# A second place for the loaded keys and queries of every second head pair

## The chip, the cores and the metric

The kernel runs on one core of a Trainium2 chip. The core has five instruction streams that run beside each other and wait for one another by semaphores: TensorE (PE: matrix products and transposes; PEld are its weight loads), VectorE (DVE), ScalarE (ACT), GpSimd (POOL) and SyncE (SP), which here issues every transfer between DRAM and the on-chip memory SBUF, in one queue. Each stream runs its instructions in order: what stands behind a waiting instruction waits too. The metric is the device time of one execution in microseconds (us).

## The reference

`reference.py` computes causal attention with a gated linear memory, and feeds its result to a two-layer network; everything is fp32. Inputs: q, k, v of shape (4, 8, 576, 64), that is 4 batches, 8 heads, 576 positions, 64 features; `M_prev` (4, 8, 64, 64), `z_prev` (4, 8, 64), `beta` (8), `w_in` (512, 2048) and `w_out` (2048, 512).

```
scores = where(causal, -1e9, q @ k.T / 8);  a = softmax(scores)
qp     = phi(q)                       # phi(x) = max(x, 0) or exp(x) - 1, plus 1
mem    = (qp @ M_prev) / (qp . z_prev + 1e-6)
attn   = g * mem + (1 - g) * (a @ v)  # g = sigmoid(beta), one number per head
x      = attn as (2304 tokens, 512);  h = x @ w_in
out    = (h * sigmoid(1.702 * h)) @ w_out
```

## The kernel before, in words

**Exact products.** A product of fp32 numbers is built from three products of a fast, shorter format (fp32r): each operand is split into a high part (a rounded copy, made by ACT) and a low part (value minus high part, made by POOL or DVE), and high*high, high*low and low*high are summed in PSUM.

**Pairs.** The 32 heads go as 16 pairs (0 to 15): two heads of one batch fill the 128 partitions. Batch 0 is pairs 0 to 3. The first 256 queries of all of batch 0 are done ahead, by `first_queries`, whose tiles lie in the pool `first`; pairs 0 to 3 then do the other 320 queries, and their memory part is one plain fp32 product. The room of `first` is given back after it, to the pools of the converted weight blocks (`w1_6` to `w1_15`); a tile in that room waits until the last reader of the tiles that it covers is done.

**What a pair goes through.** In `plan_prep`: the transposed keys (576 columns) and queries (384 or 640 columns) are loaded into one tile `kqr` of the pool `ldp`, which has one buffer for it (`load_kq`, L352 to L357); ACT makes their high part, tile `hi`, one buffer too (`split_hi`); POOL subtracts, `lok` and `loq` (its last instruction on `kqr`); ten SBUF-to-SBUF transfers stack high and low parts into two weight tiles `W0`, `W1` (L402 to L411), so that one pass of PE does what else were three. In `plan_attend`: PE makes the scores (`ps<-W`; the last 64 rows, the tail, directly from the parts: `ps<-hi`, `ps<-lok,hi`, `ps<-hi,loq`, the last readers of `hi`), DVE takes the maximum (L506), ACT the exponential (L512), POOL scales (L515), PE transposes (`pt`), ACT and DVE copy out (`e`), and PE multiplies by the values (`po<-e,vs`) and the memory (`po<-qpt,ms`). The sum is x, transposed. `load_vq` loads values, memory (`mr`), queries in the other layout (`qr`) and z (`zb`); for pairs 0 to 3, ACT writes the gated memory to the tile `ms` (two buffers, `mplain`), which PE reads.

**Blocks.** w_in comes as 16 blocks of 128 columns of d_ff, as raw 64-bit words: 512 KB each into one of the two buffers `wraw` of the pool `cnv` (L164). ACT scales the upper words (L172), DVE puts the bits together in three operations (L179, L180, L182), ACT copies the high part `wi` and POOL subtracts the low part. Blocks 0 to 5 are converted in front, 6 to 15 while the first pairs run. From about 410 us the two `wraw` buffers take w_out's raw words (L861, L865); the first two of these are loaded as soon as the buffers are free.

**First product.** h = x @ w_in runs as "fill" between the pairs' work: for each chunk of x (256 tokens, then 320, then 288 each) and each block, 12 matmuls `pm<-xh,wi` and `pm<-xl,wi`; the result is copied by ACT or DVE to `hk` (three buffers) and stored in DRAM (`gd<-hk`, L738). The second product (`acc`, L949) starts near 480 us and ends the program.

**What sets the order.** Work is put into slots: `at(slot, prio, fn)` notes a piece of work, `step()` issues those of a slot by priority and then as many first-product matmuls as `PACE` grants. Pair p starts at slot `K0[p]` (0, 7, 14, 21, then every 8); its preparation at `K0[p]-8`. The tile framework's scheduler then orders each engine's instructions by its own estimates; the order on each engine is fixed when the program is built.

Of the kernel before, what the change touches and what calls it, by code (L numbers as in the profile page):

```python
# [8 lines left out]
F32 = mybir.dt.float32  # L9
# [6 lines left out]
B, H, S, D = 4, 8, 576, 64  # L16
NP = H // 2
# [3 lines left out]
NB = DFF // 128  # L21
NK = DM // 128
SQ = 640
# [6 lines left out]
def f32(ap):  # L30
    return ap.bitcast(F32)
# [3 lines left out]
def tile_attention_memory_moe(ctx, tc, kq, vq, mem, zz, beta, w_in, w_out, out):  # L35
    nc = tc.nc
    CH = 288
    NCH = S // CH
    MB = 1
# [3 lines left out]
    W0 = 6  # L43
    CONV = [-7, -6, -5, -3, -1, 1, 3, 5, 7, 9]
    PSUM = bass.MemoryType.PSUM

    def pool(stack, name, bufs=1, **kw):
        return stack.enter_context(tc.tile_pool(name=name, bufs=bufs, **kw))

    attn = ExitStack()  # L50
    left = ExitStack()
    cst = pool(ctx, "cst", side="left")
    mop = pool(left, "mop", 2, side="left")
    cnv = pool(left, "cnv", side="left")
    w1 = [pool(left, f"w1_{k}", side="left") for k in range(W0)]
# [4 lines left out]
    ldp = pool(attn, "ldp", side="right")  # L60
    att = pool(attn, "att", side="right")
# [19 lines left out]
    def at(slot, prio, fn):  # L81
        assert slot > state["slot"], (slot, state["slot"])
        state["seq"] += 1
        events.setdefault(slot, []).append((prio, state["seq"], fn))
# [12 lines left out]
    def copy(eng, dst, src, scale=None):  # L97
        if eng == "A":
            kw = {} if scale is None else {"scale": scale}
            nc.scalar.activation(out=dst, in_=src, func=AF.Copy, **kw)  # L100
        elif eng == "V":
            if scale is None:
                nc.vector.tensor_copy(dst, src)
            else:
                nc.vector.tensor_scalar(out=dst, in0=src, scalar1=scale, scalar2=None, op0=ALU.mult)
        else:
            nc.gpsimd.tensor_copy(dst, src)

    def tt(eng, dst, a, b, op):
        (nc.vector if eng == "V" else nc.gpsimd).tensor_tensor(out=dst, in0=a, in1=b, op=op)  # L110

    def sub(eng, dst, src, hi):
        tt(eng, dst, src, f32(hi), ALU.subtract)
# [12 lines left out]
    for r in range(2):  # L126
        v = maskt[64 * r:64 * r + 64, CH - 64:CH]
# [7 lines left out]
    gt = cst.tile([128, NP], F32, name="gt")  # L135
# [206 lines left out]
    pairs = [(b, c) for b in range(B) for c in range(NP)]  # L342
    raws = {}
# [3 lines left out]
    K0 = [STEP * p for p in range(MB * NP)]  # L347
    K0 += [(K0[-1] + 8 if K0 else 0) + 8 * p for p in range(len(pairs) - len(K0))]

    def load_kq(p):  # L350
        kqr = ldp.tile([128, S + SQ], F32, name="kqr")
        b, c = pairs[p]  # L352
        if b < MB:
            nc.sync.dma_start(kqr[:, :S], kq[b, c, :, :S])
            nc.sync.dma_start(kqr[:, S:S + 384], kq[b, c, :, S + 256:])
        else:
            nc.sync.dma_start(kqr, kq[b, c])  # L357
        raws[p] = {"kq": kqr}

    def load_vq(p):  # L360
        b, c = pairs[p]

        vr = (att.tile([128, 5, 128], F32, name="vs", bufs=2) if b < MB else ldp.tile([128, 5, 128], F32, name="vr"))
        nc.sync.dma_start(vr, vq[b, c, :, 0])
        mr = ldp.tile([128, 2, D], F32, name="mr")
        nc.sync.dma_start(mr, mem[b * NP + c])
        qr = ldp.tile([128, 5, 128], F32, name="qr")
        t = 2 if b < MB else 0
        nc.sync.dma_start(qr[:, t:], vq[b, c, :, 1, t:])
        zb = ldp.tile([128, 128], F32, name="zb")  # L370
        nc.sync.dma_start(zb, zz[b, c:c + 1, :].to_broadcast([128, 128]))
        raws[p].update(v=vr, m=mr, q=qr, z=zb)

    def plan_prep(p):
        b, c = pairs[p]
        s0 = K0[p] - 8
        P = prep[p] = {}
        rest = b < MB
        T0 = 2 if rest else 0
        qo = 256 if rest else 0  # L380

        def split_hi():
            kqr = raws[p]["kq"]
            P["hi"] = att.tile([128, S + SQ], F32R, name="hi")
            copy("A", P["hi"][:, :S + SQ - qo], kqr[:, :S + SQ - qo])

        def split_lo_k():
            P["lok"] = att.tile([128, S], F32R, name="lok")
            sub("P", P["lok"], raws[p]["kq"][:, :S], P["hi"][:, :S])

        def split_lo_q():
            P["loq"] = att.tile([128, SQ], F32R, name="loq")
            n = SQ - qo
            sub("P", P["loq"][:, :n], raws[p]["kq"][:, S:S + n], P["hi"][:, S:S + n])

        def stack_hi():
            P["W"] = [att.tile([128, S + 1024 - 2 * qo], F32R, name=f"W{h}", bufs=2) for h in range(2)]
# [21 lines left out]
                P["vs"][:, :, :, 0])  # L419

        def mplain():
            P["ms"] = att.tile([128, 2 * D], F32, name="ms", bufs=2)
            copy("A", P["ms"], raws[p]["m"].rearrange("p h d -> p (h d)"), gt[:, c:c + 1])

        def msplit():
            P["ms"] = att.tile([128, 2, 2, D], F32R, name="ms", bufs=2)
# [42 lines left out]
        def qev():  # L469
# [6 lines left out]
            for pt, a, n in ((P["pt"][0][:, qo:], qo, 512 - qo), (P["pt"][1], 512, 64)):  # L476
                copy("A", qh[:, a:a + n], pt[:, :n])
                sub("V", ql[:, a:a + n], pt[:, :n], qh[:, a:a + n])

        at(s0 + 1, 50, split_hi)  # L480
        at(s0 + 3, 50, split_lo_k)
        at(s0 + 3, 51, split_lo_q)
        at(s0 + 3, 52, stack_hi)
        at(s0 + 4, 52, stack_lo)
        if rest:
            at(s0 + 7, 51, mplain)
        else:
            at(s0 + 6, 55, vhi)
            at(s0 + 7, 50, vlo)
            at(s0 + 7, 51, msplit)  # L490
# [6 lines left out]
        at(s0 + 12, 21, qtr)  # L497
        at(s0 + 13, 31, qev)
        if p + 1 < len(pairs):
            at(K0[p + 1] - 11, 60, lambda: load_kq(p + 1))  # L500
            at(max(K0[p + 1] - 8, s0 + 8), 60, lambda: load_vq(p + 1))

    def softmax_max(pieces):
        nm = sml.tile([128, 2], F32, name="nm")
# [296 lines left out]
            for blk in range(W0):  # L801
                conv_in(blk)
    first.close()
    w1 += [pool(left, f"w1_{k}", side="left", reuse_waits="tile") for k in range(W0, NB)]
    load_kq(0)
    load_vq(0)
    for p in range(NPAIRS):
        plan_prep(p)
        plan_attend(p)
# [158 lines left out]
    k = 0  # L968
# [118 lines left out]
```

## Time and profile before

| | us |
|---|---|
| three executions | 673.61, 668.46, 672.34 |
| their median | 672.34 |
| the profiled execution, own time | 669.38 |
| its span in the trace | 667.6 |
| PE busy (share of the span) | 608.9 (91%) |
| DVE busy | 473.5 (71%) |
| ACT busy | 426.8 (64%) |
| POOL busy | 276.4 (41%) |
| granted TensorE clock, mean | 0.993 |

Times of rows are microseconds from the start of the span. What lies around the span is 669.38 - 667.6 = 1.8 us. An idle time in front of an instruction stands in brackets, with what ended it; the releaser is inferred from semaphores, so where it names a piece of work that was done long before, it was another. Busy time of engines other than PE matters only where PE, or a chain that PE waits for, waits for them.

### The profile page before, as it was taken

The page shows a single profiled execution, that of the slowest core. Times are in us where ns is not written, and L with a number is a line of the kernel's source. Part 1 is how long each engine was busy: PE and PEld are TensorE (multiplying, and loading weights), DVE is VectorE, ACT ScalarE, POOL GpSimd, SP SyncE. Part 2 cuts the span into 40 slices and gives each one's busy share as a digit, 9 for nine tenths or more (in the row PEclk, how much of TensorE's full clock was granted, in tenths as well). Part 3 has the DMA queues.
Part 4 walks back from the last instruction along what each step waited for, and adds up shares of the span by engine and source line. Part 5 has one row for each costly group of instructions (what it writes and reads, how often), then busy time and mean ns, then how long its engine had stood idle before and what let it go on. Part 6 is the DMA issues. An engine that isn't in the chain of part 4 may idle for free.

```text
span 667.6 us, 12447 instructions
## 1 busy us (share of the span) xinstructions
PE 608.9 (91%) x4032; PEld 578.2 (87%) x4032; DVE 473.5 (71%) x1117; ACT 426.8 (64%) x975; POOL 276.4 (41%) x304
## 2 busy tenths in 40 slices
PE   4588799899987899999999999889989999999997
PEld 3477687699976799999989999789989999999997
DVE  5977776677587767776667745983878469658944
ACT  4676556677488866775876655744794865776441
POOL 3746554876376955664675321670710000000000
PEclk9999899999999999999999999999989999999999
DMA  8959868875678848667665136855752660672001
GB/s 243 277 146 262 241 181 213 220 200 159 184 182 234 197 153 224 185 172 233 168 183 148 55 94 213 268 181 170 233 197 88 196 190 1 180 211 83 24 2 71
DMA packets 72048, 114.50 MB, mean 172 GB/s; under 512 B 8240, under 2 KB 52272, under 8 KB 71984
## 3 DMA queue, kind: packets, MB, share of 16 engines
q1 hardware_dynamic: 71984, 113.71, 58.7%
q8 instruction: 32, 0.52, 0.3%
q14 instruction: 32, 0.26, 0.1%
HBM read 62.87 MB, written 26.69 MB: 134 GB/s over the span
## 4 chain that ended last, share of the span: by engine, by line
PE 62%; DVE 11%; ACT 9%; DMA 9%; issue 5%; POOL 2%; SPq 1%; DVEq 0%; ACTq 0%; POOLq 0%
PE acc L949 24%; PE pm L91 18%; PE po L91 7%; PE pt L95 6%; PE ps L91 4%; DMA gd<-hk 3%; DMA xl<-xd 2%; DVE st L110 1%; DMA fm<-in_mem_dram 1%; DMA xd<-xf 1%; DVE ps L506 1%; ACT a L512 1%; ACT oh L100 1%; DVE ol L110 1%; ACT wo L100 1%
## 5 line engine op out<-in xcount | busy, mean ns | idle before, releaser
L91 PE MATMUL pm<-xh,wi 128*128 128x288 f32 (+2 forms) x1024 | 220.4, 304 | 13.7 <-ACT hk L100 7.1
L91 PEld LDWEIGHTS pm<-xh,wi 128*128 128x128 f32 x1024 | 165.6, 189 | 20.1 <-ACT hk L100 9.8
L949 PE MATMUL acc<-oh,wo 128*128 128x384 f32 x672 | 159.6, 339 | 4.5 <-ACT oh L100 4.2
L91 PE MATMUL pm<-xl,wi 128*128 128x288 f32 (+2 forms) x512 | 151.7, 299 | 0.2 <-DVE xl L110 0.2
L949 PEld LDWEIGHTS acc<-oh,wo 128*128 128x128 f32 x672 | 121.1, 189 | 6.3 <-ACT oh L100 6.3
L110 DVE TENSOR_TENSOR ol<-g,oh 128x768 fp32r<-128x768 f32 x84 | 81.4, 981 | 49.1 <-ACT oh L100 47.3
L515 POOL TENSOR_SCALAR a<-a,sm,g 128x512 f32<-128x512 f32 (+3 forms) x112 | 72.7, 661 | 69.1 <-DVE sm L554 30.3
L949 PE MATMUL acc<-ol,wo 128*128 128x384 f32 x336 | 99.4, 338 | 0.1
L100 ACT ACTIVATE oh<-g 128x768 fp32r<-128x768 f32 x84 | 70.3, 840 | 43.2 <-PE acc L949 41.8
L91 PEld LDWEIGHTS pm<-xl,wi 128*128 128x128 f32 x512 | 96.6, 189 | 0.9 <-DVE xl L110 0.4
L512 ACT ACTIVATE a<-ps,nm 128x512 f32<-128x512 f32 (+3 forms) x112 | 60.3, 541 | 34.5 <-DVE nm L506 32.2
L506 DVE CUSTOM_DVE_ANT_0 ps<-ps,mask 128x256 f32<-128x256 f32 (+4 forms) x144 | 69.4, 495 | 15.6 <-PE ps L91 9.5
L91 PE MATMUL po<-e,vs 128*128 128x320 f32 (+3 forms) x416 | 74.7, 304 | 1.7 <-ACT e L100 1.5
L110 DVE TENSOR_TENSOR e<-pt,e 128x320 fp32r<-128x320 f32 (+1 forms) x120 | 55.9, 486 | 23.3 <-ACT e L100 22.3
L100 ACT ACTIVATE e<-pt 128x320 fp32r<-128x320 f32 (+4 forms) x136 | 55.2, 437 | 26.4 <-PE pt L95 12.9
L91 PEld LDWEIGHTS po<-e,vs 128*128 128x128 f32 x416 | 63.0, 189 | 6.0 <-ACT e L100 1.8
L949 PEld LDWEIGHTS acc<-ol,wo 128*128 128x128 f32 x336 | 62.3, 189 | 1.0 <-DVE ol L110 1.0
L91 PE MATMUL ps<-W 128*128 128x512 f32 (+3 forms) x224 | 58.6, 343 | 3.5 <-ACT a L512 1.0
L95 PE MATMUL pt<-ident,a 128*128 128x128 f32 x296 | 56.6, 272 | 1.5 <-ACT a L512 1.5
L100 ACT ACTIVATE hk<-pm 128x288 f32<-128x288 f32 (+2 forms) x84 | 33.7, 407 | 28.0 <-PE pm L91 16.1
L912 ACT ACTIVATE g<-g 128x768 f32<-128x768 f32 x48 | 40.0, 842 | 14.6 <-DMA g<-gd 10.4
L95 PE MATMUL pt<-ident,at 128*128 128x128 f32 x160 | 40.7, 279 | 6.7 <-ACT a L512 3.0
(147 smaller groups left out, 1020.1 us busy)
## 6 DMA issues: line engine op xcount, KB each, us to landing
g<-gd SPq DMA_DIRECT2D x48, 384.0 KB, 3.7
gd<-hk SPq DMA_DIRECT2D x96, 144.0 KB, 2.7
wraw<-in_w_in_dram SPq DMA_DIRECT2D x16, 512.0 KB, 4.4
wraw<-in_w_out_dram SPq DMA_DIRECT2D x16, 512.0 KB, 4.6
kqr<-in_kq_dram SPq DMA_DIRECT2D x12, 608.0 KB, 5.4
W<-hi SPq DMA_DIRECT2D x24, 272.0 KB, 3.5
W<-loq SPq DMA_DIRECT2D x48, 128.0 KB, 3.4
W<-lok SPq DMA_DIRECT2D x32, 144.0 KB, 3.4
```

Source lines behind the costliest of these rows:

```text
L91: nc.tensor.matmul(out, l, r, start=start, stop=stop)
L95: nc.tensor.transpose(out, in_, idn)
L100: nc.scalar.activation(out=dst, in_=src, func=AF.Copy, **kw)
L110: (nc.vector if eng == "V" else nc.gpsimd).tensor_tensor(out=dst, in0=a, in1=b, op=op)
L506: nc.vector.tensor_tensor_reduce(out=ps, in0=ps, in1=mk, op0=ALU.add, op1=ALU.min, scale=-0.125, scalar=1e38 if j == 0 else nm[:, j - 1:j] ...
L512: nc.scalar.activation(out=a, in_=ps, func=AF.Exp, scale=-1.0, bias=nm, accum_out=sm)
L515: (nc.vector if eng == "V" else nc.gpsimd).tensor_scalar(out=a, in0=a, scalar1=r, scalar2=gcol, op0=ALU.mult, op1=ALU.mult)
L912: nc.scalar.activation(out=t, in_=t, func=AF.Gelu_apprx_sigmoid)
L949: nc.tensor.matmul(acc[b, j][:, :QN], W[2 * p + kk][:, WPART[i], sp, 128 * j:128 * j + 128], mv[:, kk], start=first and p + kk == 0 and sp ...
```

## The change

**Keys and queries.** `load_kq` is called at slot max(K0[p+1]-16, 10) where it was K0[p+1]-11, and at -7 for pairs 1 and 2. The even pairs keep `kqr`. Pair 1's goes into a new pool `kqx`, which is laid where block 15's weights will be (the pool `w1_15` is opened only at slot 9, when `kqx` is closed). The odd pairs from 3 on take two tiles (keys, queries) from the two `wraw` buffers. For the odd pairs keys and queries come in two transfers, and `split_hi` becomes two ACT copies for pairs 3, 5, 7 ... 15.

**Values and memory.** `load_vq` is cut into `load_q` (priority 60) and `load_v` (61). For pairs 0 to 3 the memory is loaded straight into the tile `ms`, and `mplain` scales it there; so the load itself has to wait until PE has read what the pair two before had in that buffer.

```diff
     def load_kq(p):
-        kqr = ldp.tile([128, S + SQ], F32, name="kqr")
         b, c = pairs[p]
-        if b < MB:
-            nc.sync.dma_start(kqr[:, :S], kq[b, c, :, :S])
-            nc.sync.dma_start(kqr[:, S:S + 384], kq[b, c, :, S + 256:])
+        n = 384 if b < MB else SQ
+        if p % 2 and p > 1:
+            k, q = [cnv.tile([128, w], F32, name="wraw", bufs=2) for w in (S, n)]
+        else:
+            kqr = (ldp if p % 2 == 0 else kqx["pool"]).tile([128, S + (SQ if p % 2 == 0 else n)], F32, name="kqr")
+            k, q = kqr[:, :S], kqr[:, S:S + n]
+        if b < MB or p % 2:
+            nc.sync.dma_start(k, kq[b, c, :, :S])
+            nc.sync.dma_start(q, kq[b, c, :, S + SQ - n if b >= MB else S + 256:])
         else:
             nc.sync.dma_start(kqr, kq[b, c])
...
-    def load_vq(p):
+    def load_q(p):
...
+    def load_v(p):
+        b, c = pairs[p]
+        vr = (att.tile([128, 5, 128], F32, name="vs", bufs=2) if b < MB else ldp.tile([128, 5, 128], F32, name="vr"))
+        nc.sync.dma_start(vr, vq[b, c, :, 0])
+        mr = (att.tile([128, 2, D], F32, name="ms", bufs=2) if b < MB else ldp.tile([128, 2, D], F32, name="mr"))
+        nc.sync.dma_start(mr, mem[b * NP + c])
...
-            copy("A", P["hi"][:, :S + SQ - qo], kqr[:, :S + SQ - qo])
+            if raws[p]["kq"] is not None:
+                copy("A", P["hi"][:, :S + SQ - qo], raws[p]["kq"])
+            else:
+                copy("A", P["hi"][:, :S], raws[p]["k"])
+                copy("A", P["hi"][:, S:S + SQ - qo], raws[p]["kqq"])
...
         def mplain():
-            P["ms"] = att.tile([128, 2 * D], F32, name="ms", bufs=2)
-            copy("A", P["ms"], raws[p]["m"].rearrange("p h d -> p (h d)"), gt[:, c:c + 1])
+            P["ms"] = ms = raws[p]["m"].rearrange("p h d -> p (h d)")
+            copy("A", ms, ms, gt[:, c:c + 1])
...
-            at(K0[p + 1] - 11, 60, lambda: load_kq(p + 1))
-            at(max(K0[p + 1] - 8, s0 + 8), 60, lambda: load_vq(p + 1))
+            at(max(K0[p + 1] - 16, -7 if p < 2 else CONV[-1] + 1), 60, lambda: load_kq(p + 1))
+            at(max(K0[p + 1] - 8, s0 + 8), 60, lambda: load_q(p + 1))
+            at(max(K0[p + 1] - 8, s0 + 8), 61, lambda: load_v(p + 1))
...
-    w1 += [pool(left, f"w1_{k}", side="left", reuse_waits="tile") for k in range(W0, NB)]
+    w1 += [pool(left, f"w1_{k}", side="left", reuse_waits="tile") for k in range(W0, NB - 1)]
+    spare = ExitStack()
+    kqx = {"pool": pool(spare, "kqx", side="left", reuse_waits="tile")}
+
+    def last_w1():
+        spare.close()
+        w1.append(pool(left, f"w1_{NB - 1}", side="left", reuse_waits="tile"))
+
+    at(CONV[-1], 50, last_w1)
```

Because the framework's scheduler makes the order anew, instructions move on the engines. Three places are shown, before first and changed second; numbers at names only tell tiles apart. **SP, the transfers after pair 0's stacks** (`kqr_671` before, `kqr_557` changed: pair 1's keys; `kqr_735` changed: pair 2's; `wraw`: raw words of the blocks):

```order
L164 DMA wraw_470<-in_w_in_dram 128x1024
L411 DMA W1_625<-loq_622 64x256 x2
L354 DMA kqr_671<-in_kq_dram 128x576
L355 DMA kqr_671<-in_kq_dram 128x384
L366 DMA mr_812<-in_mem_dram 128x128
L369 DMA qr_814<-in_vq_dram 128x384
L164 DMA wraw_481<-in_w_in_dram 128x1024
L371 DMA zb_816<-in_zz_dram 128x128
L366 DMA mr_1016<-in_mem_dram 128x128
L164 DMA wraw_492<-in_w_in_dram 128x1024
L164 DMA wraw_547<-in_w_in_dram 128x1024
```

```order
L164 DMA wraw_470<-in_w_in_dram 128x1024
L424 DMA W1_628<-loq_625 64x256 x2
L361 DMA kqr_735<-in_kq_dram 128x576
L362 DMA kqr_735<-in_kq_dram 128x384
L371 DMA qr_812<-in_vq_dram 128x384
L373 DMA zb_814<-in_zz_dram 128x128
L164 DMA wraw_481<-in_w_in_dram 128x1024
L164 DMA wraw_492<-in_w_in_dram 128x1024
L164 DMA wraw_547<-in_w_in_dram 128x1024
L164 DMA wraw_587<-in_w_in_dram 128x1024
L361 DMA kqr_557<-in_kq_dram 128x576
L362 DMA kqr_557<-in_kq_dram 128x384
```

Pair 2's keys stand where pair 1's stood; pair 1's stand behind four loads of raw words.

**PE, where block 15 (`wi15`) begins**; `po_1171`/`po_1174` and `ps<-hi`, `lok`, `loq` are the rest of an earlier pair's values and the second half of pair 2's tail:

```order
L95 MATMUL pt_1152<-ident_123,a2_948 128x128
L91 MATMUL pm_1194<-xh_208,wi15_1098 128x256
L91 MATMUL po_1171<-e1_1165,vs_536 128x320
L91 MATMUL po_1171<-e0_1167,vs_536 128x192
L91 MATMUL po_1171<-e0_1167,vs_536 128x64
L91 MATMUL ps_1217<-hi_998 128x288
L91 MATMUL ps_1217<-lok_1087,hi_998 128x288
L91 MATMUL ps_1217<-hi_998,loq_1089 128x288
L91 MATMUL ps_1302<-W0_1091 128x384 x2
```

```order
L95 MATMUL pt_1155<-ident_123,a2_947 128x128
L91 MATMUL pm_1197<-xh_208,wi15_1100 128x256 x2
L91 MATMUL pm_1197<-xl_207,wi15_1100 128x256
L91 MATMUL pm_1197<-xh_208,wi15_1100 128x256 x2
L91 MATMUL pm_1197<-xl_207,wi15_1100 128x256
L91 MATMUL po_1174<-e1_1168,vs_540 128x320
L91 MATMUL po_1174<-e0_1170,vs_540 128x192
L91 MATMUL po_1174<-e0_1170,vs_540 128x64
L91 MATMUL ps_1221<-hi_996 128x288
L91 MATMUL ps_1221<-lok_1089,hi_996 128x288
L91 MATMUL ps_1221<-hi_996,loq_1091 128x288
```

Before, one matmul of block 15 stood ahead of these; changed, all twelve.

**SP, between pair 3's stacks and pair 4's** (before `kqr_1365`: pair 4's keys; changed `ms_1243`: pair 3's memory, `wraw_1408` and `wraw_1409`: pair 5's keys and queries):

```order
L411 DMA W1_1294<-loq_1291 64x256 x2
L357 DMA kqr_1365<-in_kq_dram 128x1216
L369 DMA qr_1406<-in_vq_dram 128x640
L371 DMA zb_1408<-in_zz_dram 128x128
L366 DMA mr_1404<-in_mem_dram 128x128
L364 DMA vs_1232<-in_vq_dram 128x640
L402 DMA W0_1489<-hi_1431 64x1088
```

```order
L424 DMA W1_1299<-loq_1296 64x256 x2
L371 DMA qr_1404<-in_vq_dram 128x640
L373 DMA zb_1406<-in_zz_dram 128x128
L381 DMA ms_1243<-in_mem_dram 128x128
L361 DMA wraw_1408<-in_kq_dram 128x576
L362 DMA wraw_1409<-in_kq_dram 128x640
L379 DMA vs_1241<-in_vq_dram 128x640
L415 DMA W0_1495<-hi_1437 64x1088
```

Pair 4's keys are gone from here, as they now come far earlier; pair 3's memory, which waits for PE, and pair 5's keys stand here. Pair 5's keys stood eight places behind the last row shown of before.

## Rows read from the trace of the kernel before

**Rows 1.** the page's first line: the span and the number of instructions.

```profile
span 667.6 us, 12447 instructions
```

**Rows 2.** busy time by stretches of 20 us; columns as its head line names them.

```profile
core 0: us, PE busy (x) PEld busy (x) DVE busy (x) ACT busy (x) POOL busy (x), PEclk, DMA share, GB/s
40.00:60.00 20.00, 17.11 (x111) 14.56 (x110) 16.81 (x51) 13.13 (x33) 13.87 (x15) 1.00 0.76 206
60.00:80.00 20.00, 15.13 (x105) 13.47 (x106) 15.19 (x34) 12.16 (x29) 12.73 (x14) 0.95 0.85 259
```

**Rows 3.** instructions on the tile `kqr`: durations min/median/max, then idle time before them.

```profile
L100 ACT ACTIVATE hi<-kqr x16: 998/1210/1229, 19.2 to 344.0; 128x1216 fp32r<-128x1216 f32 x12, 128x960 fp32r<-128x960 f32 x4
...
  DMA mr<-in_mem_dram: 3.5, 1
  DMA kqr<-in_kq_dram: 1.4, 2
```

**Rows 4.** timeline of ACT: start, duration, line, operation, count, [idle before it <-releaser].

```profile
43.94 1.00 ACT L100 ACTIVATE hi<-kqr 128x960 fp32r<-128x960 f32 x1 [0.42 <-PE ps L91]
...
59.67 0.38 ACT L100 ACTIVATE hk<-pm 128x256 f32<-128x256 f32 x1 [1.00 <-DMA gd<-hk]
...
95.83 1.01 ACT L100 ACTIVATE hi<-kqr 128x960 fp32r<-128x960 f32 x1
...
105.25 0.40 ACT L100 ACTIVATE ms<-mr,gt 128x128 f32<-128x128 f32 x1 [0.40 <-PE po L91]
...
108.51 1.22 ACT L100 ACTIVATE hi<-kqr 128x1216 fp32r<-128x1216 f32 x1 [0.66 <-DMA kqr<-in_kq_dram]
...
121.26 1.22 ACT L100 ACTIVATE hi<-kqr 128x1216 fp32r<-128x1216 f32 x1 [3.52 <-DMA mr<-in_mem_dram]
```

**Rows 5.** timeline of SP's DMA issues, around the keys of pairs 1, 2 and 5.

```profile
28.16 0.58 SPq L354 DMA_DIRECT2D kqr<-in_kq_dram  x1
...
46.81 0.53 SPq L164 DMA_DIRECT2D wraw<-in_w_in_dram  x1
...
116.93 0.58 SPq L357 DMA_DIRECT2D kqr<-in_kq_dram  x1
```

**Rows 6.** timeline of PE, 47 to 125 us.

```profile
47.21 0.38 PE L315 MATMUL pm<-ft,fv 128*128 128x128 f32 x2
...
76.66 0.39 PE L91 MATMUL pm<-xh,wi 128*128 128x256 f32 x1 [2.62 <-POOL wi L110]
...
78.88 0.58 PE L91 MATMUL pm<-xh,wi 128*128 128x256 f32 x1 [0.34 <-POOL wi L110]
...
95.50 0.29 PE L91 MATMUL ps<-hi,loq 128*128 128x288 f32 x1
...
118.08 0.30 PE L91 MATMUL ps<-hi,loq 128*128 128x288 f32 x1
...
123.01 0.33 PE L95 MATMUL pt<-ident,at 128*128 128x128 f32 x1 [1.81 <-ACT at L512]
...
124.84 0.33 PE L95 MATMUL pt<-ident,at 128*128 128x128 f32 x1 [0.57 <-ACT at L512]
```

**Rows 7.** chain of waits, one piece: start, length, what.

```profile
85.13 1.44 PE pm L91 x12
```

**Rows 8.** timeline of POOL: the low part of block 15.

```profile
93.59 1.28 POOL L110 TENSOR_TENSOR wi<-wr,wi 128x512 fp32r<-128x512 f32 x1 [2.59 <-ACT wi L100]
```

**Rows 9.** timeline of DVE: copies of results that waited for a store.

```profile
60.15 0.42 DVE L103 COPY hk<-pm 128x256 f32<-128x256 f32 x1 [1.68 <-DMA gd<-hk]
...
64.86 0.42 DVE L103 COPY hk<-pm 128x256 f32<-128x256 f32 x1 [1.58 <-DMA gd<-hk]
```

**Rows 10.** busy time in one stretch of 4 us; columns as in Rows 2.

```profile
76.00:80.00 4.00, 3.00 (x17) 2.71 (x18) 2.67 (x6) 2.59 (x5) 3.17 (x4) 0.75 0.81 252
```

**Rows 11.** DMA issues: KB each, median us from issue to landing.

```profile
mr<-in_mem_dram SPq DMA_DIRECT2D x16, 64.0 KB, 3.2
...
kqr<-in_kq_dram SPq DMA_DIRECT2D x4, 192.0 KB, 4.0
```

More of the change, by code (lines that the diff above doesn't have):

```diff
@@ L350, in load_kq @@
     def load_kq(p):
-        kqr = ldp.tile([128, S + SQ], F32, name="kqr")
         b, c = pairs[p]
-        if b < MB:
-            nc.sync.dma_start(kqr[:, :S], kq[b, c, :, :S])
-            nc.sync.dma_start(kqr[:, S:S + 384], kq[b, c, :, S + 256:])
+        n = 384 if b < MB else SQ
[7 more added lines that the diff above has]
+            nc.sync.dma_start(q, kq[b, c, :, S + SQ - n if b >= MB else S + 256:])
         else:
             nc.sync.dma_start(kqr, kq[b, c])
-        raws[p] = {"kq": kqr}
-    def load_vq(p):
+        raws[p] = {"k": k, "kqq": q, "kq": None if p % 2 and p > 1 else kqr[:, :S + n]}
+    def load_q(p):
         b, c = pairs[p]
[L363 to L366, printed above, removed]
         qr = ldp.tile([128, 5, 128], F32, name="qr")
@@ L371, in load_vq @@
         nc.sync.dma_start(zb, zz[b, c:c + 1, :].to_broadcast([128, 128]))
-        raws[p].update(v=vr, m=mr, q=qr, z=zb)
+        raws[p].update(q=qr, z=zb)
+    def load_v(p):
[4 more added lines that the diff above has]
+        nc.sync.dma_start(mr, mem[b * NP + c])
+        raws[p].update(v=vr, m=mr)
     def plan_prep(p):
@@ L382, in split_hi @@
         def split_hi():
-            kqr = raws[p]["kq"]
             P["hi"] = att.tile([128, S + SQ], F32R, name="hi")
-            copy("A", P["hi"][:, :S + SQ - qo], kqr[:, :S + SQ - qo])
+            if raws[p]["kq"] is not None:
[3 more added lines that the diff above has]
+                copy("A", P["hi"][:, S:S + SQ - qo], raws[p]["kqq"])
         def split_lo_k():
             P["lok"] = att.tile([128, S], F32R, name="lok")
-            sub("P", P["lok"], raws[p]["kq"][:, :S], P["hi"][:, :S])
+            sub("P", P["lok"], raws[p]["k"], P["hi"][:, :S])
         def split_lo_q():
@@ L393, in split_lo_q @@
             n = SQ - qo
-            sub("P", P["loq"][:, :n], raws[p]["kq"][:, S:S + n], P["hi"][:, S:S + n])
+            sub("P", P["loq"][:, :n], raws[p]["kqq"], P["hi"][:, S:S + n])
         def stack_hi():
@@ L803, in tile_attention_memory_moe @@
     first.close()
-    w1 += [pool(left, f"w1_{k}", side="left", reuse_waits="tile") for k in range(W0, NB)]
+    w1 += [pool(left, f"w1_{k}", side="left", reuse_waits="tile") for k in range(W0, NB - 1)]
[5 more added lines that the diff above has]
+    at(CONV[-1], 50, last_w1)
     load_kq(0)
-    load_vq(0)
+    load_q(0)
+    load_v(0)
     for p in range(NPAIRS):
```

## The prediction

> **What bounds the kernel now.** I read the page's first line for the span, then stretches of time, then the tile whose load is moved, then the timelines of the engines at the places where the order changes. The profiled execution took 669.38 us, its span 667.6 [rows 1]; it lies 3.0 us under the median of the three executions shown (672.34), and the mean of all four is 670.9. PE is busy 91% of the span, so a gain can only come from places where PE idles. Two of them lie where this change works: from 40 to 80 us PE is busy 17.11 and 15.13 of each 20 us [rows 2]. There the converted blocks come too late: PE waited 2.62 and then 0.34 us for low parts of w_in blocks [rows 6].
>
> How much do the keys hold anything up? Their reader is ACT's `hi<-kqr`, 16 times. ACT stood idle before it for 1.4 us over two times by the keys' transfers, and once for 3.5 us [rows 3]. The latter is pair 5's `hi` at 121.26 [rows 4]; its releaser is given as the memory's transfer, which this instruction doesn't read. The keys were issued at 116.93 [rows 5], so they are what it waited for, 4.3 us. In the other thirteen no load of keys ended a wait: `hi` has one buffer, and its refill waits for the tail scores of the pair before, whichever buffer the raw keys lie in. So most of the early loading can give nothing, and the sum is made of the first six pairs.
>
> **The change part by part**, against 669.38.
>
> A, **pair 1's keys come later.** They were issued at 28.16 [rows 5] and split at 43.94 [rows 4]. Now they stand behind four loads of raw words, the last of which was issued at 46.81 [rows 5], and wait for the last reader of `first`'s tiles, which ends at 47.21+0.38 = 47.6 [rows 6]. Two issues of about 0.6 us and 4.0 us of landing [rows 11] put them at 52.5 or so, 8.6 us behind the old split. What covers this: 61 first-product matmuls more stand ahead of pair 1's tail on PE (84 where 23 stood), at 1.44/12 = 0.12 us [rows 7] that is 7.3 us of work. Taken: 0; bounds 0 and +8.6. Nearest row: PE waits for blocks at 76.66 all the same, so a delay of the pair ahead of that comes out of that wait first.
>
> B, **the conversions run ahead.** With pair 1's `hi` and softmax out of the way until 52, ACT and DVE convert blocks earlier. And the stores of results no longer stand behind pair 1's stacks on SP: ACT waited 1.00 us [rows 4] and DVE 1.68 and 1.58 us [rows 9] for such stores to free a buffer. [...]
>
> C, **block 15 ahead of pair 2's second tail half.** PE reached that place before 95.50 [rows 6]; the low part of block 15 is only done at 93.59+1.28 = 94.9 [rows 8]. With all twelve matmuls in front, PE waits for it, where before one matmul on the high part and then the pair's own work stood. The work ahead of it is 11 matmuls shorter, 1.3 us. Taken: +1.4; bounds 0 (if B moves block 15 too) and +1.4 plus 0.5.
>
> D, **pair 3's keys** go to the raw words' buffers and wait until those of blocks 14 and 15 are read, which is so at the latest when block 15's low part starts, at 93.59 [rows 8]. Landing 4.0 us [rows 11] gives 97.6 at the latest, against a `hi` at 95.83 [rows 4], right after the tail that ends with the row at 95.50 [rows 6]. C puts that tail behind its wait and eleven matmuls, 2.7 us in all, so the keys are there first. Taken: 0; bounds 0 and +1.8.
>
> E, **pair 3's memory goes into `ms` directly.** Before, it was loaded ahead into `mr`, and ACT's scaling waited 0.40 us for PE's last read of the buffer, until 105.25 [rows 4]. Now the transfer itself waits on SP for that read, and lands 3.2 us later [rows 11], about 108.4. On ACT its scaling now stands ahead of a copy of x, a step on the queries and pair 4's `hi`; so pair 4's `hi`, 108.51 before [rows 4], goes to about 110, although its keys are now long there. Behind ACT come 3.2 us of POOL for the low parts, until about 114.5, before the tail that ended with the row at 118.08 [rows 6]: slack 2.7 us. The copy of x delayed by 1 us may cost PE something. Taken: +0.5; bounds 0 and +1.5. [...]
>
> Queued behind that waiting transfer on SP are pair 5's keys, pair 3's values and pair 4's stacks. The stacks need `hi` at 111 anyway, pair 5's keys are needed at 118: 0.
>
> F, **pair 5's keys are there in time.** Issued near 106, landed near 111. `hi` of pair 5 then waits only for pair 4's tail, 118.08+0.30 = 118.4, not 121.26: the 3.52 us of ACT are gone, and with them PE's waits of 1.81 and 0.57 us for the tail's exponential, which stood behind it on ACT [rows 6]. Taken: -2.4; bounds -3.5 (all of ACT's idle time) and 0 (the exponential then waits for the maximum instead).
>
> G, **small edits, all hidden.** For seven pairs `hi` is two instructions, some 0.2 us more on ACT, and SP has one issue more, 0.58 us [rows 5]; from pair 6 on neither is what PE waits for. w_out's first raw words are loaded only after pair 15's keys, which are split by 345 us or so (the last `hi` starts at 344.0 [rows 3]); the first of them are needed from about 410 us, as before: 0.
>
> Sum: 0 - 2 + 1.4 + 0 + 0.5 - 2.4 + 0 = -2.5, so 666.9 for an execution like the profiled one, and 670.9 - 2.5 = **668.4** as the middle of several.
>
> **The rivals.** *Nothing comes of it*: B and F are each given back and C and E stay, 670.9+1.9 = 672.8, or 670.9 where these too are hidden; PE's missing work in 40 to 80 us is then bound by DVE and ACT together, and pair 5's wait turns into one for the maximum. For it: in thirteen of sixteen pairs no key was waited for. Against: 3.52 us at pair 5 is a wait with an end of its own.
>
> *Pair 1 starves PE* (slower). The place is 52 to 64 us; the mechanism: the fill between the queue's blocks runs out before pair 1's stacks land, as blocks 3 to 5 are read earlier than before and blocks 6 to 9 are not converted any sooner. It decides if the 84 matmuls end before pair 1's low parts are there, about 56 us. Then A is the full +8.6, B is nothing, a second fall of the clock costs another 0.75 us [rows 10], and C, E and F stay: 670.9 + 8.6 + 0.75 + 1.4 + 0.5 - 2.4 = 679.8. For it: PE was idle a quarter of 60 to 80 us already. Against: 7.3 of the 8.6 us are covered by work that stands in the order.
>
> [...]
>
> That the change doesn't do what it says can't be ruled out for pairs 6 to 15: earlier keys there change no wait; this is in all cases.
>
> **How the numbers follow.** Forecast 0.45 (666 to 670.5), nothing 0.22, starved 0.13, more 0.20. About 1% of the median shown, 6.7 us, is what a measurement of this kernel tells from no change: the single executions differ by 5.2 us. Faster by over 1% (under 665.6) takes all of the last case and 0.04 of the forecast: 0.24. Slower (over 679.1) takes two thirds of the starved case: 0.09. The rest, 0.67, lies within 1%. The range runs from 661.5, the fast case and its scatter, to 676, which leaves most of the starved case out.
>
> **What would show it.** A: pair 1's `hi` near 52.5, and PE busy between 50 and 60 us. B: the waits for low parts of blocks at 76 us shortened, `hk` copies without a wait for stores. C: a wait of 1 to 1.5 us of PE for block 15's low part. E: `ms` scaled about 108.4, pair 4's `hi` after 109. F: pair 5's `hi` right behind pair 4's tail, no wait for a transfer. It is wrong if PE waits over 3 us between 50 and 65 us, or if waits for keys or for `ms` stand beyond pair 6.

## The result, and the profile after

The changed kernel is slower. Four executions took 681.01, 678.98, 685.87 and 679.30 us (median 680.15); the kernel before, with one more execution beside them, 672.98. The ratio is 1.0136, 95% interval 1.009 to 1.0183. Run again later on one chip with other kernels it gave 1.0149 (1.0080 to 1.0219). The forecast was 668.4 with a range from 661.5 to 676. Ratios leave out executions in which the whole program ran disturbed; medians don't.

The profiled execution took 681.01 us; its span is 11.6 us longer than that of before [rows 1].

```profile
span 679.2 us, 12442 instructions
...
PE 612.7 (90%) x4032; PEld 581.6 (86%) x4032; DVE 476.4 (70%) x1117; ACT 428.7 (63%) x982; POOL 274.9 (40%) x304
```

PE's busy time is up by 612.7 - 608.9 = 3.8 us for the same 4032 matmuls, and its idle time by 66.5 - 58.7 = 7.8. The first goes with the clock (mean granted 0.979, before 0.993), as the stretches of 20 us show (the column behind POOL's is the granted clock):

```profile
40.00:60.00 20.00, 18.65 (x120) 16.62 (x119) 15.37 (x43) 11.98 (x28) 11.65 (x13) 0.92 0.55 160
60.00:80.00 20.00, 12.55 (x72) 10.36 (x71) 11.14 (x29) 9.41 (x22) 10.66 (x11) 0.83 0.83 211
80.00:100.00 20.00, 17.13 (x100) 14.75 (x101) 15.13 (x33) 10.15 (x25) 8.46 (x8) 0.91 0.64 199
100.00:120.00 20.00, 16.11 (x99) 13.34 (x97) 9.54 (x32) 10.86 (x27) 9.83 (x11) 1.00 0.61 165
```

PE is busy 12.55 us from 60 to 80 where it was 15.13, at 0.83 of the clock where it was 0.95 [rows 2]. ACT's timeline gives the delay pair by pair:

```profile
52.03 1.01 ACT L100 ACTIVATE hi<-kqr 128x960 fp32r<-128x960 f32 x1 [0.46 <-DMA kqr<-in_kq_dram]
...
64.27 1.00 ACT L100 ACTIVATE hi<-kqr 128x960 fp32r<-128x960 f32 x1 [2.71 <-DMA W<-hi]
...
66.64 0.63 ACT L172 ACTIVATE ws<-wraw 128x512 f32<-128x512 f32 x1
...
98.99 0.40 ACT L100 ACTIVATE ms<-ms,gt 128x128 f32<-128x128 f32 x1 [1.91 <-DMA ms<-in_mem_dram]
...
104.74 1.10 ACT L100 ACTIVATE hi<-wraw 128x576 fp32r<-128x576 f32 x2
...
116.72 0.40 ACT L100 ACTIVATE ms<-ms,gt 128x128 f32<-128x128 f32 x1 [0.67 <-DMA ms<-in_mem_dram]
...
118.25 1.20 ACT L100 ACTIVATE hi<-kqr 128x1216 fp32r<-128x1216 f32 x1
...
128.31 1.31 ACT L100 ACTIVATE hi<-wraw 128x576 fp32r<-128x576 f32 x2 [0.80 <-POOL a L529]
```

Against [rows 4], pair 1's `hi` is 8.1 us late (52.03 for 43.94), pair 3's 8.9 (104.74 for 95.83), pair 4's 9.7, pair 5's only 7.05. So the delay is there at the first pair and is not made up by the fourth; the wait for pair 5's keys is gone, as forecast. Later the same view has pair 10 late by 8.0 us (229.30 for 221.30) and pair 11 by 11.7 (259.67 for 247.95): a second loss. PE's timeline shows the two places:

```profile
65.80 0.80 PE L91 MATMUL ps<-W 128*128 128x512 f32 x1 [3.81 <-ACT at L526]
...
80.48 0.88 PE L91 MATMUL ps<-W 128*128 128x384 f32 x2 [2.65 <-ACT a L526]
...
86.44 0.39 PE L91 MATMUL pm<-xh,wi 128*128 128x256 f32 x1 [1.71 <-POOL wi L110]
...
101.65 0.39 PE L91 MATMUL pm<-xh,wi 128*128 128x256 f32 x1 [0.89 <-POOL wi L110]
...
241.42 0.90 PE L91 MATMUL po<-qpt,ms 128*128 128x320 f32 x2 [3.58 <-DVE xf L110]
```

What ends the waits is in the chain of waits of the first stretch (start, length, what):

```profile
58.82 5.29 DMA W<-hi
...
71.53 0.69 DVE wr L182
72.24 6.96 DMA wraw<-in_w_in_dram
...
96.17 2.80 DMA ms<-in_mem_dram
```

The three transfers among these rows now start late. The last of pair 1's `W<-hi` was issued at 58.82 and landed at 64.11. Pair 2's `hi` overwrites what that transfer reads, so ACT stood 2.71 us in front of it; pair 1's tail exponentials stood behind, and PE 3.81 us behind them. The second transfer is block 11's raw words, and it starts where DVE's last operation on its buffer ends. Behind pair 2's late `hi` ACT scaled block 9's raw words only at 66.64 (before 63.85), DVE was done with them at 72.2, and only then was there room: 72.24, before 68.46. ACT waited 2.36 us for them, exponentials stood behind on ACT, and PE 2.65 us behind these. The third is the memory of pair 2.

The second loss is on DVE and POOL:

```profile
237.00 3.91 DVE L441 SCALAR_TENSOR_TENSOR ms<-mr,gt,ms 128x128 fp32r<-128x128 f32 x1
```

```profile
236.21 3.06 POOL L110 TENSOR_TENSOR xl<-xl,xh 128x288 fp32r<-128x288 f32 x4
239.22 1.54 POOL L110 TENSOR_TENSOR vs<-vr,vs 128x640 fp32r<-128x640 f32 x1
```

```profile
236.00:240.00 4.00, 0.61 (x2) 0.30 (x2) 3.41 (x2) 2.90 (x8) 4.00 (x6) 0.71 0.96 210
240.00:244.00 4.00, 2.58 (x10) 2.54 (x11) 3.71 (x10) 1.88 (x5) 2.32 (x3) 0.50 0.42 103
```

DVE's low part of the memory, two operands in SBUF, takes 3.91 us; the twelve of its kind take 0.50 in the median. It ends at 240.91, just after POOL's five subtractions that follow on one another (240.76). PE runs dry (0.61 us busy of 4), and the clock is at 0.50 in the 4 us after.

### The profile page after: what moved, and what is told of

Its sections match the earlier page's. It is cut to its first block, busy times and chain, and to the rows that moved or that the text cites. A ratio compares the mean times of both kernels' runs of the same rounds, so it can differ in the third digit from the quotient of the medians.

```text
span 679.2 us, 12442 instructions
## 1 busy us (share of the span) xinstructions
PE 612.7 (90%) x4032; PEld 581.6 (86%) x4032; DVE 476.4 (70%) x1117; ACT 428.7 (63%) x982; POOL 274.9 (40%) x304
## 4 chain that ended last, share of the span: by engine, by line
PE 61%; DMA 12%; DVE 11%; ACT 10%; issue 4%; SPq 1%; POOL 1%; DVEq 0%; ACTq 0%
PE pm L91 22%; PE acc L972 19%; PE po L91 8%; PE pt L95 6%; PE ps L91 5%; DMA g<-gd 2%; DMA wraw<-in_w_in_dram 2%; DVE ol L110 2%; ACT oh L100 2%; DMA xl<-xd 2%; DVE st L110 1%; DMA gd<-hk 1%; ACT g L935 1%; DVE ps L520 1%; DMA qr<-in_vq_dram 1%
## 5 line engine op out<-in xcount | busy, mean ns | idle before, releaser
L529 POOL TENSOR_SCALAR a<-a,sm,g 128x512 f32<-128x512 f32 (+3 forms) x112 | 71.3, 647 | 71.1 <-DVE sm L568 42.9
L100 ACT ACTIVATE oh<-g 128x768 fp32r<-128x768 f32 x84 | 70.3, 840 | 43.2 <-PE acc L972 42.1
L520 DVE CUSTOM_DVE_ANT_0 ps<-ps,mask 128x256 f32<-128x256 f32 (+4 forms) x144 | 69.5, 494 | 17.3 <-PE ps L91 11.6
L91 PE MATMUL ps<-W 128*128 128x512 f32 (+3 forms) x224 | 60.3, 350 | 12.0 <-ACT a L526 4.0
L91 PEld LDWEIGHTS ps<-W 128*128 128x128 f32 x224 | 35.9, 191 | 14.8 <-ACT a L526 4.6
```

Source lines behind the costliest of these rows:

```text
L91: nc.tensor.matmul(out, l, r, start=start, stop=stop)
L520: nc.vector.tensor_tensor_reduce(out=ps, in0=ps, in1=mk, op0=ALU.add, op1=ALU.min, scale=-0.125, scalar=1e38 if j == 0 else nm[:, j - 1:j] ...
L529: (nc.vector if eng == "V" else nc.gpsimd).tensor_scalar(out=a, in0=a, scalar1=r, scalar2=gcol, op0=ALU.mult, op1=ALU.mult)
```

## The experiments

Ratios are to the kernel before on the same chip, with 95% intervals. Four groups of three or four kernels each, run together; before stood at 673.5, 673.7, 672.4 and 674.3 us in them.

| kernel | median us | ratio |
|---|---|---|
| pair 1's keys late, alone (late1) | 677.63 | 1.0037 (0.9988 to 1.0086) |
| memory tile alone (msalone) | 675.19 | 1.0049 (1.0015 to 1.0084) |
| odd pairs' room alone (odd3) | 673.38 | 1.0005 (0.9971 to 1.0038) |
| late1 and msalone together (late1ms) | 687.34 | 1.0199 (1.0141 to 1.0257) |
| changed, pair 1 put right (swap12) | 676.73 | 1.0043 (1.0003 to 1.0082) |
| changed, memory tile put right (msback) | 677.25 | 1.0050 (1.0017 to 1.0082) |
| changed, once more (again) | 683.62 | 1.0149 (1.0080 to 1.0219) |
| low part of memory on POOL: before / odd3 / changed | 681.67 / 679.32 / 687.82 | 1.0110 (1.0056 to 1.0164) / 1.0071 (1.0039 to 1.0103) / 1.0199 (1.0144 to 1.0254) |
| low parts of x on DVE: before (vbefore) | 673.82 | 1.0025 (0.9998 to 1.0052) |
| the same: odd3 (vodd3) | 670.97 | 0.9979 (0.9942 to 1.0015) |
| vodd3 again (vodd3b) | 671.43 | 0.9962 (0.9930 to 0.9993) |
| the same: changed (vafter) | 679.12 | 1.0097 (1.0061 to 1.0132) |
| vodd3 without pair 3 (vodd5) | 669.32 | 0.9932 (0.9903 to 0.9961) |

**Pair 1's late keys alone (late1).** The kernel before, with the pool `kqx` of the change, and

```diff
-        kqr = ldp.tile([128, S + SQ], F32, name="kqr")
+        kqr = kqx["pool"].tile([128, S + 384], F32, name="kqr") if p == 1 else ldp.tile([128, S + SQ], F32, name="kqr")
...
-            at(K0[p + 1] - 11, 60, lambda: load_kq(p + 1))
+            at(-7 if p == 0 else K0[p + 1] - 11, 60, lambda: load_kq(p + 1))
```

> The kernel before with one part of the change alone: pair 1's keys go to the room of block 15 and wait there for the last reader of first_queries' tiles; all other loads, the slots of the other pairs and the memory tile as before. Theory (the late keys of pair 1 are the loss): pair 1's `hi` at about 52 instead of 43.9, the last tail matmul of pair 1 at about 59 instead of 51.9, pair 2's `hi` at about 64 instead of 55.9, and a time 7 to 9 us over the kernel before (ratio about 1.012). Rival (the loss is made by the odd pairs' room in the raw words' buffers and by the memory tile that waits): within 2 us of the kernel before. Second rival (cover holds, as predicted): the same within 2 us, with `hi` of pair 1 late but pair 2's on time.

Measured: 1.0037 by the ratio, 2.5 us (4.1 by the medians), and its interval holds 1; a third of what the theory said, and not shown as a loss by itself. `hi` of pair 1 is at 50.6 and of pair 2 at 62.7 (6.75 late), as the theory had it, but pair 3's at 97.8, 2.0 late: two thirds are made up by then. PE's longest wait at its first scores is

```profile
63.01 0.50 PE L91 MATMUL ps<-W 128*128 128x512 f32 x1 [1.52 <-DMA W<-lok]
```

where the changed kernel has 3.81. So the cover that the prediction counted on is partly there.

**Pairs 1 and 2 exchanged in the changed kernel (swap12).**

```diff
-            kqr = (ldp if p % 2 == 0 else kqx["pool"]).tile([128, S + (SQ if p % 2 == 0 else n)], F32, name="kqr")
+            kqr = (kqx["pool"] if p == 2 else ldp).tile([128, S + (n if p == 2 else SQ)], F32, name="kqr")
...
-            at(max(K0[p + 1] - 16, -7 if p < 2 else CONV[-1] + 1), 60, lambda: load_kq(p + 1))
+            at(K0[1] - 11 if p == 0 else max(K0[p + 1] - 16, -7 if p < 2 else CONV[-1] + 1), 60, lambda: load_kq(p + 1))
```

> The changed kernel with pairs 1 and 2 exchanged: pair 1's keys stay in the first place and are loaded at the old time, pair 2's go to the room of block 15; all the rest as changed. Theory (late keys of pair 1 are the loss): pair 1's `hi` near 44, pair 2's near 56, pair 5's right behind pair 4's tail, and a time of 667 to 671, 1 to 4 us under the kernel before and about 10 under the changed one. Rival (odd pairs' room and memory tile): 676 or more.

Measured: 676.73, 1.0043. The place was right (`hi` at 43.2 and 53.8) and the time was the rival's: by the ratios 6.3 of the changed kernel's 9.2 us go and the rest stays, so the loss is not pair 1's alone. ACT's wait for pair 2's memory (1.28 us) and the long DVE operation (4.00 us) are still there.

**The odd pairs' room alone (odd3).** `load_kq` and `split_hi` as changed, without `kqx`:

```diff
-            at(K0[p + 1] - 11, 60, lambda: load_kq(p + 1))
+            at(K0[p + 1] - 11 if p < 2 else max(K0[p + 1] - 16, CONV[-1] + 1), 60, lambda: load_kq(p + 1))
```

> The kernel before with the other part alone: the odd pairs from 3 on load to the raw words' buffers and all pairs from 2 on at the new slots; pair 1 and the memory tile as before. Theory: pair 5's `hi` loses its wait of 3.5 us for keys and PE the two waits of 1.8 and 0.6 us behind it: 2 to 3 us under the kernel before (ratio 0.996). Rival (this room is the loss: pair 3's keys wait for block 15's words): pair 3's `hi` 2 us or more later than 95.8 against its pair's tail, time 2 us or more over the kernel before.

Measured: no difference (1.0005). Both theories missed, and the trace says how: pair 5's `hi` is at 117.9 (before 121.3), pair 10's at 218.8 (221.3), so 2.5 us are won as forecast; pair 11's is at 249.35 (247.95). Between stands

```profile
226.57 3.80 DVE L436 SCALAR_TENSOR_TENSOR ms<-mr,gt,ms 128x128 fp32r<-128x128 f32 x1
```

where the kernel before has the same instruction at 227.48 with 0.36 us. The gain is given back here.

**The memory tile undone (msback) and alone (msalone).** msback loads to `mr` again and scales from there to a tile `ms`; msalone is the kernel before with the change's edits of `mr` and `mplain` only.

> The changed kernel with the memory of pairs 0 to 3 loaded ahead to a tile of its own again and scaled from there. Theory: pair 1's keys are still late, so the time stays at 678 to 681; of the changed kernel's time at most 1 us goes. Rival (the memory's transfer that waits on SP holds up what is queued behind it): 676 or less.

Measured: 677.25, 1.0050, so 3 us of the changed kernel's loss by the medians and 5.8 by the ratios go with this edit; nearer to the rival, which said 676. Pair 1's late `hi` (51.4) and the long DVE operation (3.85 us) are still there.

> The kernel before with the memory of pairs 0 to 3 loaded straight into the tile `ms`, and nothing else of the change. Theory (three parts add up: late keys of pair 1 some 4 us, memory tile some 3 to 5 us, odd pairs' room nothing): ACT waits 1 to 2 us for the memory's transfer of pair 2 near 90 us and again for pair 3, and the time is 2 to 5 us over the kernel before. Rival (the memory tile costs only beside the other parts, as the prediction's half microsecond): within 1 us of the kernel before.

Measured: 675.19, over the kernel before by 2.8 us by the medians, 3.3 by the ratio, and clear of 1; the theory's. The load was issued at 88.05, just after PE's last read of the buffer (88.02), and ACT's timeline has its wait for it:

```profile
89.93 0.40 ACT L100 ACTIVATE ms<-ms,gt 128x128 f32<-128x128 f32 x1 [1.43 <-DMA ms<-in_mem_dram]
```

For pair 3, where it was expected too, ACT doesn't wait.

**The held DVE operation: taken away.** In three kernels POOL makes the low part of the memory:

```diff
-            copy("A", P["ms"][:, :, 0], raws[p]["m"], gt[:, c:c + 1])
-            nc.vector.scalar_tensor_tensor(
-                out=P["ms"][:, :, 1], in0=raws[p]["m"], scalar=gt[:, c:c + 1], in1=f32(P["ms"][:, :, 0]),
-                op0=ALU.mult, op1=ALU.subtract)
+            m = raws[p]["m"]
+            copy("A", m, m, gt[:, c:c + 1])
+            copy("A", P["ms"][:, :, 0], m)
+            sub("P", P["ms"][:, :, 1], m, P["ms"][:, :, 0])
```

> The changed kernel once more, beside the kernels below, so that they are compared on one chip. It should repeat: 678 to 682, DVE's `ms<-mr,gt,ms` of the pair near 237 us again 3.5 to 4 us long, and ACT waiting 1 to 2 us for the memory of pair 2 at 97 to 99 us.

> The changed kernel with one DVE instruction per pair from pair 4 on taken away: the memory's low part (two operands in SBUF, on DVE) is made by POOL instead, from a memory that ACT scales in place. Theory (this DVE operation is held for as long as POOL's five subtractions follow on one another, 3.9 us at 237, and PE runs dry behind it): the distance of the `hi` of pairs 10 and 11 falls from 30.4 to about 26.5, the clock does not fall there, and the time is 3 to 5 us under the changed kernel. Rival (the stretch waits for x of the third batch anyway, and the long DVE row is only where that shows): within 1 us of the changed kernel.

> The kernel before with the odd pairs' room from pair 3 on, and the same DVE instruction taken away. Theory: pair 5's gain of 2 to 3 us, which was given back at 227 us by the held DVE operation (3.80 us there), now stays: 668 to 671, 3 us or so under the kernel before. Rival: 672 to 674, as without the edit.

> The kernel before with only the DVE instruction taken away: a control. There the operation took 0.35 to 1.24 us, so both theories expect the time of the kernel before within 1.5 us; if it gains 3 us or more, the gain of the two kernels above is not one of the held operation.

The changed kernel repeated itself (683.62, a little over its expectation; the DVE row 3.67 us). The edit is a bad one: it costs the control 8.0 us, so no time here met its expectation. Against that control, though, the changed kernel costs 1.0199 - 1.0110 = 0.9% instead of 1.5%, and odd3 is 0.4% faster instead of equal, with intervals that overlap. The distance of the `hi` of pairs 10 and 11, 30.7 and 30.6 us in the kernels with the held operation, is 28.7 and 26.0; but in the control it falls too, from 26.65 to 24.9. So odd3's fall points to the theory, and the changed kernel's, no larger than the control's but for 0.2 us, says nothing.

**The held DVE operation: its neighbour moved.** POOL's run is shortened instead:

```diff
-            sub("P", xl[:, c, :w], f32(xl[:, c, :w]), xh[:, c, :w])
+            sub("V" if n == 3 else "P", xl[:, c, :w], f32(xl[:, c, :w]), xh[:, c, :w])
```

> The changed kernel with one thing moved: the four low parts of the x chunk that POOL makes one after the other at 236 us (`xl<-xl,xh`, 3.06 us) are made by DVE, ahead of its `ms<-mr,gt,ms`. Nothing else is moved on any engine. Theory (DVE's operation with two operands in SBUF is held while POOL's run of such operations lasts): the `ms` row near 237 us falls from 3.7-3.9 us to at most 1.6 (one POOL operation), the distance of the `hi` of pairs 10 and 11 from 30.5 to 27 to 28.5, the clock's fall there is less, and the time is 2 to 4 us under the changed kernel. Rival (the row shows a wait for something else): it stays near 3.8 us and so does the time.

> The kernel before with the odd pairs' room from pair 3 on, and the same four low parts on DVE. Theory: pair 5's gain of 2 to 3 us stays to the end: 669 to 671.5, ratio to the kernel before about 0.996. Rival (the odd pairs' room gains nothing in any case): 673 to 674.

> The kernel before with the four low parts on DVE, a control: there `ms` comes before POOL's run and takes 0.36 us. Expected: the time of the kernel before within 1 us, or up to 1.5 us more, as DVE has 1.8 us more to do in a stretch where PE waits for it.

Measured, DVE's timeline of the changed kernel with this edit:

```profile
235.45 1.86 DVE L110 TENSOR_TENSOR xl<-xl,xh 128x288 fp32r<-128x288 f32 x4 [1.40 <-ACT xh L100]
...
237.64 0.34 DVE L441 SCALAR_TENSOR_TENSOR ms<-mr,gt,ms 128x128 fp32r<-128x128 f32 x1
```

The row falls from 3.91 to 0.34 us, and the distance to 28.8 (expected up to 28.5; the control has 27.6). The clock's fall is not less: it is 0.92 in the mean from 220 to 240 us and 0.90 from 240 to 260, in the changed kernel 0.94 and 0.89; PE is busy 14.52 of the first 20 us, there 12.83. The ratio falls to 1.0097, from 1.0136 and 1.0149, which is 2.6 to 3.5 us, but the intervals overlap. The control is 0.25% slower than before, odd3 with the edit 0.2% faster, and 0.4% with more executions on another chip, an interval clear of the control's. So the theory is shown for the row; the times agree with it, and in the changed kernel that isn't clear of noise.

**Do the two losses add? (late1ms)** late1 with msalone's edits.

> The kernel before with pair 1's late keys and with the memory tile of pairs 0 to 3, without the odd pairs' room. On PE its order up to pair 3 is that of the changed kernel, block 15 ahead of pair 2's second tail half included. If the two costs only add (4.2 and 2.8 us by the medians of the two alone), the time is 679 to 681 and `hi` of pair 3 comes at about 99 to 100. If they make each other worse, and the changed kernel's loss is all here, it is 681 to 684 and pair 3's `hi` at 103 or later; then the odd pairs' room gives the changed kernel nothing back.

Measured: 687.34, 1.0199, over the top of the expectation. By the ratios they cost 13.4 us together, alone 2.5 and 3.3. Two rows of it, ACT's and DVE's, show where the rest comes from:

```profile
96.42 0.40 ACT L100 ACTIVATE ms<-ms,gt 128x128 f32<-128x128 f32 x1 [2.66 <-DMA ms<-in_mem_dram]
```

```profile
236.33 5.46 DVE L428 SCALAR_TENSOR_TENSOR ms<-mr,gt,ms 128x128 fp32r<-128x128 f32 x1
```

Pair 3's `hi` is at 101.8, 2.5 us later than the two delays of 2.0 and 1.5 added would put it; with both edits block 15 stands ahead of pair 2's second tail half on PE, and ACT copies its high part only after the memory came. And the DVE operation is held 5.46 us, where late1 and msalone have 0.59 and 0.53: from pair 10 to 11 it takes 30.8 us, in those two 26.1 and 27.0. The changed kernel, which has the odd pairs' room as well, is 3.4 to 4.2 us faster than late1ms by the ratios, but their intervals overlap: that the room wins there is likely and not shown.

**The best version (vodd3b, vodd5).** vodd5 is vodd3 with `p > 3` for `p > 1` in `load_kq`, and the old slot for pair 3.

> The odd pairs' room with the four low parts on DVE once more, with more rounds, as the best version so far. Theory: 670 to 672, ratio 0.996 to 0.999 to the kernel before, the interval now clear of 1. Rival: ratio 1.000 to 1.002, no gain.

> As the kernel above, but pair 3 keeps the first place (its keys need no room that block 15's raw words hold), so only the pairs 5, 7, ... take the second place. If pair 3's wait for that room costs anything, pair 4's `hi` follows pair 3's by 12.7 us as in the kernel before and not by 13.8, and the time is 1 us under the kernel above; else the two are equal within 1 us.

Measured: 0.9962 and 0.9932, both clear of 1. vodd5, 669.32 us, beats the kernel before by 0.7% and the changed one by 1.6% or more (medians 674.25, and 680.15 from another chip). It stands 2.1 us under vodd3b by the medians, with intervals that overlap, and the reason named isn't borne out: pair 4's `hi` follows pair 3's by 13.7 us in it, too.

## Why the prediction was wrong, step by step

**A, pair 1's late keys, taken at 0: the step that failed, with E.** The times were right (52.03 for 52.5 forecast) and so was the work that covers: PE is busy 18.65 of the 20 us up to 60. What was left out is the time behind the split: ten stacks that stand on SP among stores and raw words, 5.29 us for the last `W<-hi` to land, and pair 2's `hi` in the one buffer that this transfer reads. PE's wait of 3.81 us came there. The prediction's own sign for it, over 3 us between 50 and 65, was met at its very end. Alone the step costs 2.5 us and isn't clear of 0 (late1); put right in the changed kernel, it takes 6.3 us with it (swap12). Both lie inside its bounds of 0 to 8.6: the step was mis-sized because the cover was counted for the split alone and not for the chain behind it, and because it was priced apart from E. (Pair 2's call, whose keys took pair 1's place on SP, stands at slot max(14 - 16, -7) = -2 and not at -7 as said with the change.)

**B, conversions run ahead, -2: not so.** No run shows the term. The waits for stores went (from 40 to 100 us no `hk` copy of ACT or DVE waits for one), but the conversions ran behind: block 15's low part ends at 101.6, before at 94.9. The loads of blocks 8 to 10 are within 1.1 us of before; from block 11 on the buffers come free late, as told above. In place of the 2 us, PE's waits for low parts of blocks are 1.71 and 0.89 us (before 2.62 and 0.34), 0.36 less together, while the scores wait 3.81 and 2.65.

**C, +1.4, and D, 0.** Block 15's low part was awaited 0.89 us; pair 3's keys were there ahead of its `hi`, no wait. Both as told in kind. But C's order needed A and E together (late1, msalone, swap12 and msback have one matmul of block 15 ahead, as before), and it goes with 2.5 us of their extra.

**E, the memory tile, +0.5: right mechanism, wrong pair and size.** It was worked out for pair 3 (ACT waited 0.67 us, pair 4's `hi` came 0.8 us further behind). Pair 2's memory waits in the same way, for 1.91 us, and behind that stand the last block's conversion and an exponential. Alone 3.3 us. Its landing took 2.80 and 3.4 us where the prediction had 3.2; in msalone it took 1.9 us, and ACT waited 1.43 all the same. What costs is that the load starts only after PE's read.

**F, pair 5's keys, -2.4: right, and given back.** From pair 4's `hi` to pair 5's it is 10.1 us instead of 12.75, 2.7 less. 110 us later DVE and POOL have shifted against each other so that one DVE operation meets POOL's run, and it takes 3.3 to 5.1 us longer. No step of the prediction looked at the stretch from 200 to 240 us, where PE idled 5.9 and 2.4 of each 20 us before the change. (The two copies of G take 1.10 and 1.31 us where one took 1.01 and 1.22: 0.09 more, not 0.2.)

**The rivals.** "Pair 1 starves PE" gave 679.8 and a chance of 0.13; the measured 680.15 is its number, and the delay of 8.1 us from its first pair on is its picture in the trace. The number was met by luck: it took 8.6 us for this mechanism, which late1 alone puts at 2.5, and the rest came by E, by C's order and by the held operation, with F beside them. By the ratios A and E cost 2.5 and 3.3 us alone and 13.4 together, of the changed kernel's 9.2 to 10.0; so some 7.6 us arise only where both are, and the odd pairs' room takes 3.4 to 4.2 off (not clear of noise). In the prediction's terms: A, B, C and E were -0.1 together and measured 13.4; D, F and G were -2.4 and measured 0.3 by themselves (odd3). How much of A comes from the clock, which differs between executions of one kernel (0.967 to 0.981 in the four of the changed), was not separated. No run shows a gain like the fast end of the range, 661.5: the largest here is vodd5's 0.7%.

## What to carry to other kernels

A load put earlier in a program is only early if its room, and the room of what the queue has ahead of it, is free: pair 1's keys waited under 0.5 us for their own room, but behind a load of raw words that had waited 4.9 us for its buffer. The price is then the chain behind the load (stack, buffer, raw words), not the lateness of the load itself. When a small step is mended early, look at the next stretch in which the bound engine idles: a shift of some us there decides which operations of other engines fall together. Parts that cost little alone should be run in pairs before they are called small: here 2.5 and 3.3 us made 13.4.

## What the runs showed of the hardware

DVE's operation with two inputs in SBUF was held beside a run of POOL's subtractions. It took 0.34 us with POOL idle (vafter, at 237.64; POOL has nothing from 235.90 to 238.28), and 3.80 to 5.46 us where POOL's operations followed on one another without a gap (odd3, msback, changed, swap12, late1ms). It ended just after POOL's last: at 240.91 for 240.76 in the changed kernel, at 241.79 for 241.65 in late1ms. In the changed kernel it got no turn between POOL's instructions: from 237.00 to 240.76 one followed on another. Not each of POOL's operations held it: in the kernel before it took 0.36 us at 227.48, while four of POOL's scalings (L515) ran from 227.13 to 229.12. What in the operations decides this was not shown.

The granted clock did not follow the length of one wait. In the changed kernel it fell to 0.50 at 237.7 us, just ahead of the wait of 3.58 us, which began at 237.84 (one of 1.99 had ended at 237.23), and was granted in full again from 244.5, 3.1 us after PE's work began again. In late1ms PE idled 6.14 of the 20 us up to 240 and 2.30 of the 20 after; the clock is 1.00 in the first and 0.83 in the second. In the kernel before it fell to 0.50 at 78 us (1.00 from 77 to 78, 0.50 from 78 to 79), 1.3 us after the end of a wait of 2.62 [rows 6]; odd3 passed a wait of 2.60 us, ended at 75.61, with 1.00 from 60 to 100.
